# Moving small bound, epsilon and fold instructions between ScalarE, VectorE and GpSimd in a top-k attention kernel with a gated feed-forward

## The chip, the cores and the metric

The kernel runs on one core of one Trainium2 chip. The metric is the time of one execution in microseconds, as the device measures it. The kernel before took 1493.38 us (the median of three runs, 1491.07 to 1494.66).

In profile lines PE is TensorE (PEld its weight loads), DVE is VectorE, ACT is ScalarE, POOL is GpSimd and SP is SyncE, which here only issues DMAs.

## The reference, cut to what matters

```python
# q, k, v: 8 batches, 8 heads, 576 positions, 64 per head (float32)
scores = scale * np.matmul(q, k.transpose(0, 1, 3, 2))       # scale = 1/8
kth = np.partition(scores, -32, axis=-1)[..., -32:-31]       # 32nd largest of each row
scores = np.where(scores >= kth, scores, -1000000000.0)
scores = scores - np.max(scores, axis=-1, keepdims=True)
attn = np.exp(scores)
attn = attn / (np.sum(attn, axis=-1, keepdims=True) + 1e-09)
attn_out = np.matmul(attn, v)
x = attn_out.transpose(0, 2, 1, 3).reshape(4608, 512)
h = x @ w_in                                                  # w_in 512 x 2048, float64
out = (h * np.cos(h)) @ w_out                                 # w_out 2048 x 512, float64
```

For each of 64 x 576 rows of scores the kernel needs two numbers: the row's largest score and its 32nd largest. The weights come as 64-bit floats, so each is two 32-bit words.

## The kernel before, in words

**Units and slots.** The 4608 rows are cut into 36 blocks of 128 tokens, and each block has four head pairs: 144 units, each a tile `s` of 128 rows x 2 heads x 576 scores. A loop over slots (line 815) issues the work by hand: in slot i unit i (`u`) is searched for its top 32, unit i-1 (`w`) is masked and exponentiated, unit i-2 (`x`) is sent through a transposing DMA, and in each second slot units i-4 and i-3 (`z`) are multiplied with v. Slots 0 to 8 are `early_slot`, which transposes on TensorE instead; slots 9 to 140 are `slot`; the rest are `last_slot`. The order in which a slot calls its functions is the order of each engine's queue.

**The search.** For all but the last two units a row is folded first: position p of the first 288 scores is paired with position p of the last 288. The larger of each pair goes to `rest` (`fold_high`, L242, VectorE, one input in PSUM), the lesser to `low`. GpSimd makes the lesser without comparing: `fold_sum` (L252) adds the two as integers and `fold_low` (L261) subtracts the larger. VectorE then takes the top 32 of `rest` in four rounds of MAX8 (L323) and MATCH_REPLACE8 (L326), and the top 16 of `low` in two rounds. In the next slot `merge_first` and `merge_second` (L311, L316) combine the two lists; after that the 32nd largest and the largest of a row stand side by side at the end of the tile `top`.

**Bounds, mask, exponentials.** `bounds(w)` on ScalarE makes `nb`, both numbers times -1/8 (L333), and `nd`, the difference of the two times 1/8 (L336, one instruction for each head). `mask` (L345) is a Prelu with bias `nb` and slope 2^100 below zero, so that every score under the 32nd largest goes far down. `exponentials` (L353) takes Exp with bias `nd` and sums each row into `den`; L358 adds 1e-9. In the next slot VectorE's `reciprocal` (L362) stands first in its queue, and GpSimd's `split` (L379, L381) copies the 16-bit halves of the exponentials and of the reciprocals to `halves`, which SP writes out (L389) and reads back transposed (L395) as `pT`. The early slots multiply by the reciprocal on GpSimd (L367) and transpose on TensorE.

**The weights.** They come in 32 chunks of 128 x 512 double words into tiles `st`, seven buffers shared with the feed-forward's `g`. `decode_first` (ScalarE) turns the high word to a float pattern (L130) and rounds the low word to an integer (L133); `decode_second` (VectorE, L141) shifts the pattern by three bits; `decode_third` (GpSimd, L151) adds the rounded low word. The last chunks are decoded in slots 9 to 13.

**The feed-forward.** `feed` puts matmuls of `ff1` (L497) and `ff2` (L572) between the attention's matmuls on TensorE, on a budget of about four groups a slot. ScalarE takes their PSUM banks (L511, L513, L582) and computes the sine (L552); GpSimd reduces and gates (L533, L542, L559). `scale_values` (L451, VectorE) multiplies the attention's output by the reciprocals in each second slot.

Of the kernel before, what the change touches and what calls it, by code (L numbers as in the profile page):

```python
# [30 lines left out]
def kernel(  # L31
# [34 lines left out]
    nc.vector.memset(halfpi, math.pi / 2.0)  # L66
    quarter = consts.tile([P, 1], F32, tag="quarter")
    nc.vector.memset(quarter, 0.25)
    eps = consts.tile([P, 1], F32, tag="eps")
    nc.vector.memset(eps, EPS)  # L70

# [52 lines left out]
    def decode_first(n):  # L124


        for _ in range(min(n, len(wq["loaded"]))):
            st, w = wq["loaded"].popleft()
            lo, hi = st[:, :, 0], st[:, :, 1]
            nc.scalar.activation(  # L130
                out=w, in_=hi.bitcast(F32), func=AF.Prelu, scale=2.0**-111, alpha=2.0**32
            )
            nc.scalar.mul(out=lo, in_=lo.bitcast(U32), mul=2.0**-29)  # L133
            wq["second"].append((st, w))

    def decode_second(n):

        for _ in range(min(n, len(wq["second"]))):
            st, w = wq["second"].popleft()
            wi = w.bitcast(I32)  # L140
            nc.vector.tensor_scalar(  # L141
                out=wi, in0=wi, scalar1=3, scalar2=None, op0=ALU.logical_shift_left
            )
            wq["third"].append((st, w))
# [92 lines left out]

    def fold_high(u):

        s, sc = u["s"], u.pop("sc")  # L240
        u["rest"] = work.tile([P, 2, S], F32, tag="rest", name="rest", bufs=1)
        nc.vector.tensor_tensor(  # L242
            out=u["rest"][:, :, HS:S], in0=sc[:, :, 0:HS], in1=s[:, :, HS:S], op=ALU.max
        )

    def fold_sum(u):

        if not u["folds"]:
            return
        s = u["s"].bitcast(I32)  # L250
        u["low"] = work.tile([P, 2, HS], F32, tag="low", name="low", bufs=1)
        nc.gpsimd.tensor_tensor(  # L252
            out=u["low"].bitcast(I32), in0=s[:, :, 0:HS], in1=s[:, :, HS:S], op=ALU.add
        )

    def fold_low(u):

        if not u["folds"]:
            return
        low = u["low"].bitcast(I32)  # L260
        nc.gpsimd.tensor_tensor(  # L261
            out=low, in0=low, in1=u["rest"][:, :, HS:S].bitcast(I32), op=ALU.subtract
        )

    tops = []
    for i in range(3):
        t = consts.tile([P, 2, TOPK, 2], F32, tag=f"top{i}", name=f"top{i}")
        nc.vector.memset(t[:, :, 0, 1], -NEG)
        tops.append(t)

# [2 lines left out]
    def topk_first(u, w):  # L273

        u["top"] = tops[u["n"] % len(tops)]
        merges = w and w["folds"]
        if merges:
            merge_first(w)
        if u["folds"]:
            fold_sum(u)  # L280
            fold_high(u)
            if u["n"] <= EARLY:
                fold_low(u)
        else:
            u["rest"] = work.tile([P, 2, S], F32, tag="rest", name="rest", bufs=1)
        if merges:
            merge_second(w)
        topk_round(u, 0)

    def topk_round(u, rnd):  # L290
# [36 lines left out]

    def bounds(u):

        ends = u.pop("top").rearrange("p j r i -> p j (r i)")  # L330
        ends = ends[:, :, 2 * TOPK - 2 :] if u["folds"] else ends[:, :, 2 * TOPK - 2 :: 2 - 2 * TOPK]
        nb = u["nb"] = small.tile([P, 2, 2], F32, tag="nb", name="nb")
        nc.scalar.mul(out=nb, in_=ends, mul=-SCALE)  # L333
        nd = u["nd"] = small.tile([P, 2], F32, tag="nd", name="nd")
        for j in range(2):
            nc.scalar.activation(  # L336
                out=nd[:, j : j + 1], in_=ends[:, j, 1:2], func=AF.Identity,
                bias=nb[:, j, 0:1], scale=SCALE,
            )

    def mask(u):

        s, nb = u["s"], u.pop("nb")
        for j in range(2):
            nc.scalar.activation(  # L345
                out=s[:, j], in_=s[:, j], func=AF.Prelu, bias=nb[:, j, 1:2], scale=SCALE, alpha=FAR
            )

    def exponentials(u):
        s, nd = u["s"], u.pop("nd")  # L350
        den = u["den"] = small.tile([P, 2], F32, tag="den", name="den")
        for j in range(2):
            nc.scalar.activation(  # L353
                out=s[:, j], in_=s[:, j], func=AF.Exp, bias=nd[:, j : j + 1], scale=1.0,
                accum_out=den[:, j : j + 1],
            )

        nc.scalar.activation(out=den, in_=den, func=AF.Identity, bias=eps, scale=1.0)  # L358

    def reciprocal(u):  # L360
        u["rden"] = small.tile([P, 2], F32, tag="rden", name="rden")
        nc.vector.reciprocal(u["rden"], u.pop("den"))  # L362

    def normalise(u):
        s, rden = u["s"], u.pop("rden")
# [293 lines left out]
    def early_slot(i, u, w):  # L659
        n = 3 if i < 6 else 2  # L660
        topk_first(u, w)
        if i == 0:
            decode_second(1)
        scores(units[i + 1])
        for load, b, hp in at_slot.get(i, []):
            load(b, hp)
        load_weights(n)
        if w:
            bounds(w)
# [24 lines left out]
        if w:  # L694
            values([w])
            take_values([w])
        feed(2)
        sines(2)
# [7 lines left out]
    def slot(i, u, w, x, z):  # L706
        if x:
            reciprocal(x)
        if u:
            topk_first(u, w)  # L710
            decode_second(2)
        if x:
            send(x)
        if u:
            fold_low(u)
            topk_round(u, 1)
            topk_round(u, 2)
            topk_round(u, 3)
        made = scored.get(i, [])
        if z:  # L720
            take_banks()
        feed(1)

        ahead = i < EARLY + 5 * NP
        if z and not ahead:
            values(z)
        for m in made:
            scores(m)
        if z and ahead:
            values(z)  # L730


        late = len(made) > 0

        decoding = i < EARLY + 8
        if i % 2 and not decoding:
            sines(1)
        if w:
            bounds(w)
# [24 lines left out]
        if decoding or i == LAST:  # L764
            sines(1)

    def last_slot(i, u, w, x, z):
        if x:
            reciprocal(x)
        if u:  # L770
            topk_first(u, w)
            fold_low(u)
            topk_round(u, 1)
        bounds(w)
# [101 lines left out]
```

## Time and profile before

| what | value |
|---|---|
| median of three runs | 1493.38 us (1491.07 to 1494.66) |
| the profiled execution's own time | 1492.78 us |
| its span, first to last instruction | 1491.0 us |
| TensorE busy | 1409.2 us, 95% of the span |
| VectorE busy | 1332.0 us, 89% |
| ScalarE busy | 1217.2 us, 82% |
| GpSimd busy | 1165.1 us, 78% |
| mean granted TensorE clock | 0.981 |

A line of the groups gives the line in the code, the engine, the operation, what it writes and reads, the number of instructions, their busy time in us and the mean ns of one, then the idle time before them and what ended it. A line of the waits reads "engine, tile and line <- what released it: us in total, times, longest". A line of the timeline gives the start in us, the length in us, engine, line and operation, and in brackets the idle time before it with its releaser. A busy share is a mean over stages, and the stages differ here: the first 235 us fill the pipeline and decode the weights, the next 1140 us repeat one pattern every two slots, and the last 115 us empty it.

### The profile page before, as it was taken

What the parts mean: (1) busy time and instruction counts of PE and PEld (TensorE: products, weight loads), DVE (VectorE), ACT (ScalarE), POOL (GpSimd) and SP (SyncE); (2) the same over time, 40 slices, a digit from 0 to 9 for tenths busy, and PEclk for the clock granted to TensorE, in tenths of its full rate; (3) what the DMA queues carried; (4) which work ended last, traced back from release to release, by engine and by line L of the source; (5) the groups of instructions that cost most, each with busy time, mean ns of one, the idle gap of its engine ahead of it and who ended that gap; (6) DMA issues with size and microseconds to landing.
All of it is one profiled execution on the core that took longest, in us unless ns stands there. A gap on an engine that the chain in (4) does not pass through costs nothing.

```text
span 1491.0 us, 30595 instructions
## 1 busy us (share of the span) xinstructions
PE 1409.2 (95%) x10360; PEld 1013.3 (68%) x10360; DVE 1332.0 (89%) x4764; ACT 1217.2 (82%) x2438; POOL 1165.1 (78%) x822
## 2 busy tenths in 40 slices
PE   5678599999999999999999999999999999999998
PEld 3456366777777777777767777677667777777665
DVE  6888899999999999999999999999999999999721
ACT  6887778888888888888888888888888888888651
POOL 5688777888888888888888888888888888888410
PEclk9888799999999999999999999999999999999999
DMA  8523476656665566556655566656765566555200
GB/s 265 159 86 101 138 203 160 156 146 187 190 165 149 149 176 192 160 151 193 180 165 149 149 179 175 171 149 160 198 170 146 149 165 181 160 147 148 70 8 15
DMA packets 405549, 229.54 MB, mean 154 GB/s; under 512 B 355088, under 2 KB 371728, under 8 KB 405392
## 3 DMA queue, kind: packets, MB, share of 16 engines
q1 hardware_dynamic: 399984, 217.93, 53.8%
q10 hardware_dynamic: 5408, 9.65, 1.8%
q8 instruction: 82, 1.34, 0.4%
q14 instruction: 75, 0.61, 0.1%
HBM read 45.09 MB, written 95.94 MB: 95 GB/s over the span
## 4 chain that ended last, share of the span: by engine, by line
PE 76%; ACT 12%; DVE 5%; DMA 4%; issue 1%; POOL 0%; SPq 0%; ACTq 0%; POOLq 0%
PE mm L497 29%; PE o L572 28%; PE rim L432 10%; PE sc L223 7%; DMA pT<-rows 2%; ACT s L353 2%; DVE top L323 2%; PE rim L223 2%; ACT s L345 2%; ACT s L233 1%; DVE rest L326 1%; ACT L353 1%; ACT L552 1%; ACT x L552 1%; DVE xT L451 1%
## 5 line engine op out<-in xcount | busy, mean ns | idle before, releaser
L497 PEld LDWEIGHTS mm<-xT,w_in 128*128 128x128 f32 x4608 | 538.2, 192 | 74.5 <-issue 51.4
L572 PE MATMUL o<-w_out,g 128*128 128x512 f32 x1152 | 540.4, 603 | 17.2 <-POOL w_out L151 13.6
L497 PE MATMUL mm<-xT,w_in 128*128 128x128 f32 x4608 | 542.1, 276 | 6.2 <-DVE xT L451 2.8
L323 DVE MAX8 top<-rest 128x8 f32<-128x288 f32 x1148 | 470.3, 451 | 0.0
L326 DVE MATCH_REPLACE8 rest<-top,rest 128x288 f32<-128x288 f32 (+1 forms) x860 | 376.3, 445 | 0.0
L252 POOL TENSOR_TENSOR low<-s 128x576 int32<-128x576 int32 x142 | 204.4, 1439 | 197.5 <-DVE top L323 81.1
L572 PEld LDWEIGHTS o<-w_out,g 128*128 128x128 f32 x1152 | 203.1, 191 | 205.0 <-issue 181.3
L379 POOL COPY halves<-s 128x2304 uint16<-128x2304 uint16 x132 | 278.1, 2107 | 0.5 <-DMA rows<-halves 0.5
L353 ACT ACTIVATE s<-s,nd 128x576 f32<-128x576 f32 x288 | 220.3, 766 | 14.0 <-ACT ob L582 13.2
L323 DVE MAX8 top<-low 128x8 f32<-128x288 f32 x568 | 229.1, 445 | 0.0
L345 ACT ACTIVATE s<-s,nb 128x576 f32<-128x576 f32 x288 | 205.3, 760 | 0.0
L261 POOL TENSOR_TENSOR low<-low,rest 128x576 int32<-128x576 int32 x142 | 201.2, 1417 | 1.8 <-DVE top L316 0.9
L432 PEld LDWEIGHTS rim<-pT,v 128*64 128x64 f32 x2560 | 135.0, 141 | 66.3 <-ACT nb L333 43.2
L432 PE MATMUL rim<-pT,v 128*64 128x128 f32 (+1 forms) x2560 | 163.9, 273 | 16.4 <-ACT pT L413 8.4
L511 ACT ACTIVATE g<-mm 128x512 f32<-128x512 f32 x144 | 84.6, 588 | 114.5 <-PE mm L497 114.5
L559 POOL TENSOR_TENSOR g<-g,x 128x1024 f32<-128x1024 f32 x68 | 160.7, 2363 | 8.2 <-ACT x L552 8.2
L542 POOL TENSOR_TENSOR x<-g,x 128x1024 f32<-128x1024 f32 x68 | 160.8, 2365 | 5.7
L223 PE MATMUL sc<-k,q 64*128 64x448 f32 (+1 forms) x640 | 155.0, 594 | 7.5 <-DVE rest L326 5.5
L233 ACT COPY s<-sc 128x896 f32<-128x896 f32 x144 | 129.8, 901 | 3.2 <-PE sc L223 3.2
L326 DVE MATCH_REPLACE8 low<-top,low 128x288 f32<-128x288 f32 x284 | 123.5, 441 | 0.0
L242 DVE TENSOR_TENSOR rest<-sc,s 128x576 f32<-128x576 f32 x142 | 106.1, 747 | 11.4 <-ACT s L234 11.4
L223 PEld LDWEIGHTS rim<-k,q 64*128 64x128 f32 (+1 forms) x640 | 59.6, 184 | 56.7 <-issue 53.4
(56 smaller groups left out, 1394.3 us busy)
## 6 DMA issues: line engine op xcount, KB each, us to landing
rows<-halves SPq DMA_DIRECT2D x132, 640.0 KB, 3.0
out_dram<-ob ACTq DMA_DIRECT2D x36, 256.0 KB, 2.1
q<-in_q_dram SPq DMA_DIRECT2D x31, 288.0 KB, 3.5
st<-in_moe_w_in_dram SPq DMA_DIRECT2D x16, 512.0 KB, 5.7
v<-in_v_dram SPq DMA_DIRECT2D x32, 256.0 KB, 3.1
st<-in_moe_w_out_dram SPq DMA_DIRECT2D x16, 512.0 KB, 4.1
k<-in_k_dram SPq DMA_DIRECT2D x31, 144.0 KB, 3.7
k<-in_k_dram SPq DMA_DIRECT2D x32, 128.0 KB, 3.6
```

The lines of the kernel that those rows point to most:

```text
L223: nc.tensor.matmul(to[r0 : r0 + rows, j, 0 : k1 - k0], st["q"][d, q0 : q0 + rows], st["k"][d, k0:k1], start=True, stop=True,)
L252: nc.gpsimd.tensor_tensor(out=u["low"].bitcast(I32), in0=s[:, :, 0:HS], in1=s[:, :, HS:S], op=ALU.add)
L261: nc.gpsimd.tensor_tensor(out=low, in0=low, in1=u["rest"][:, :, HS:S].bitcast(I32), op=ALU.subtract)
L323: nc.vector.max(to[:, j], src[:, j])
L326: nc.vector.match_replace(rest[:, j], to[:, j], src[:, j], NEG)
L345: nc.scalar.activation(out=s[:, j], in_=s[:, j], func=AF.Prelu, bias=nb[:, j, 1:2], scale=SCALE, alpha=FAR)
L353: nc.scalar.activation(out=s[:, j], in_=s[:, j], func=AF.Exp, bias=nd[:, j : j + 1], scale=1.0, accum_out=den[:, j : j + 1],)
L379: nc.gpsimd.tensor_copy(out=halves[:, :, 0 : 2 * S], in_=s.rearrange("p (k h) -> p h k", h=2))
L432: nc.tensor.matmul(o[d, to], lhsT, rhs, start=c == 0, stop=c == NT)
L497: nc.tensor.matmul(mm[:, at : at + w], w_in[f // FC][:, c, (f % FC) * P : (f % FC + 1) * P], blk["xT"][:, c], start=c == 0, stop=c == NC - 1,)
L542: nc.gpsimd.tensor_tensor(out=x, in0=g, in1=x, op=ALU.subtract)
L572: nc.tensor.matmul(o, g[:, at : at + P], w_out[f], start=f == 0, stop=f == NF - 1)
```

## The change

Five things change.

1. `bounds` moves from ScalarE to VectorE: one TENSOR_REDUCE with negation writes minus the two numbers (`less`, four values a row) behind the end of `top`, and a second adds the 32nd largest and minus the largest (`nd`). For the two unfolded units a copy of one value a head goes ahead. It is called in `topk_first`, after `merge_second`, instead of ahead of `mask`.
2. `mask` on ScalarE first multiplies `nd` by 1/8, then does its two Prelu with scale 1 and bias `less`; the factor 1/8 moves to the Exp's scale.
3. Epsilon lies beside each row's sum in three fixed tiles `dens`; VectorE's `reciprocal` adds the two by a TENSOR_REDUCE ahead of the reciprocal. ScalarE's L358 goes.
4. The low word of the weights is rounded by a GpSimd TENSOR_SCALAR in `decode_second`, instead of ScalarE's L133 in `decode_first`.
5. For units 0 to 8 the lesser scores are made by one VectorE minimum, `fold_now`, instead of GpSimd's `fold_sum` and `fold_low`.

```diff
@@ decode_first / decode_second
-            nc.scalar.mul(out=lo, in_=lo.bitcast(U32), mul=2.0**-29)
...
+            nc.gpsimd.tensor_scalar(
+                out=lo, in0=lo.bitcast(U32), scalar1=2.0**-29, scalar2=1.0, op0=ALU.mult, op1=ALU.mult
+            )
             nc.vector.tensor_scalar(
                 out=wi, in0=wi, scalar1=3, scalar2=None, op0=ALU.logical_shift_left
             )
@@ folds
+    def fold_now(u):
+        s, sc = u["s"], u.pop("sc")
+        u["low"] = work.tile([P, 2, HS], F32, tag="low", name="low", bufs=1)
+        nc.vector.tensor_tensor(
+            out=u["low"], in0=sc[:, :, 0:HS], in1=s[:, :, HS:S], op=ALU.min
+        )
...
+    dens = []
+    for i in range(3):
+        t = consts.tile([P, 2, 2], F32, tag=f"dens{i}", name=f"dens{i}")
+        nc.vector.memset(t[:, :, 1], EPS)
+        dens.append(t)
@@ topk_first
         if u["folds"]:
-            fold_sum(u)
+            if u["n"] > EARLY:
+                fold_sum(u)
             fold_high(u)
-            if u["n"] <= EARLY:
-                fold_low(u)
...
         if merges:
             merge_second(w)
+        if w:
+            bounds(w)
+        if u["folds"] and u["n"] <= EARLY:
+            fold_now(u)
         topk_round(u, 0)
@@ bounds, mask, exponentials, reciprocal
-        nc.scalar.mul(out=nb, in_=ends, mul=-SCALE)
-        nd = u["nd"] = small.tile([P, 2], F32, tag="nd", name="nd")
-        for j in range(2):
-            nc.scalar.activation(
-                out=nd[:, j : j + 1], in_=ends[:, j, 1:2], func=AF.Identity,
-                bias=nb[:, j, 0:1], scale=SCALE,
-            )
+        if not u["folds"]:
+            nc.vector.tensor_copy(out=top[:, :, end - 1], in_=top[:, :, 0])
+        u["less"] = top[:, :, end : end + 2]
+        nc.vector.tensor_reduce(
+            out=u["less"], in_=top[:, :, end - 2 : end].unsqueeze(3), axis=mybir.AxisListType.X,
+            op=ALU.max, negate=True,
+        )
+        u["nd"] = small.tile([P, 2], F32, tag="nd", name="nd")
+        nc.vector.tensor_reduce(
+            out=u["nd"], in_=top[:, :, end - 1 : end + 1], axis=mybir.AxisListType.X, op=ALU.add
+        )
...
+        nc.scalar.mul(out=u["nd"], in_=u["nd"], mul=SCALE)
         for j in range(2):
             nc.scalar.activation(
-                out=s[:, j], in_=s[:, j], func=AF.Prelu, bias=nb[:, j, 1:2], scale=SCALE, alpha=FAR
+                out=s[:, j], in_=s[:, j], func=AF.Prelu, bias=less[:, j, 1:2], scale=1.0, alpha=FAR
             )
...
-        nc.scalar.activation(out=den, in_=den, func=AF.Identity, bias=eps, scale=1.0)
...
-        nc.vector.reciprocal(u["rden"], u.pop("den"))
+        den = small.tile([P, 2], F32, tag="den", name="den")
+        nc.vector.tensor_reduce(out=den, in_=u.pop("den"), axis=mybir.AxisListType.X, op=ALU.add)
+        nc.vector.reciprocal(u["rden"], den)
```

More of the change, by code (lines that the diff above doesn't have):

```diff
@@ L68 @@
     nc.vector.memset(quarter, 0.25)
-    eps = consts.tile([P, 1], F32, tag="eps")
-    nc.vector.memset(eps, EPS)
     DECODE = moe_w_in.dtype != F32
@@ L128, in decode_first @@
             st, w = wq["loaded"].popleft()
-            lo, hi = st[:, :, 0], st[:, :, 1]
+            hi = st[:, :, 1]
             nc.scalar.activation(
@@ L139, in decode_second @@
             st, w = wq["second"].popleft()
-            wi = w.bitcast(I32)
+            wi, lo = w.bitcast(I32), st[:, :, 0]
+            nc.gpsimd.tensor_scalar(
+                out=lo, in0=lo.bitcast(U32), scalar1=2.0**-29, scalar2=1.0, op0=ALU.mult, op1=ALU.mult
+            )
             nc.vector.tensor_scalar(
@@ L238, in fold_high @@
     def fold_high(u):
-        s, sc = u["s"], u.pop("sc")
+        s, sc = u["s"], u["sc"]
+        if u["n"] > EARLY:
+            del u["sc"]
         u["rest"] = work.tile([P, 2, S], F32, tag="rest", name="rest", bufs=1)
@@ L263, in fold_low @@
         )
+    dens = []
[3 more added lines that the diff above has]
+        dens.append(t)
     tops = []
     for i in range(3):
-        t = consts.tile([P, 2, TOPK, 2], F32, tag=f"top{i}", name=f"top{i}")
+        t = consts.tile([P, 2, TOPK + 1, 2], F32, tag=f"top{i}", name=f"top{i}")
         nc.vector.memset(t[:, :, 0, 1], -NEG)
@@ L279, in topk_first @@
         if u["folds"]:
-            fold_sum(u)
+            if u["n"] > EARLY:
+                fold_sum(u)
             fold_high(u)
-            if u["n"] <= EARLY:
-                fold_low(u)
         else:
@@ L328, in bounds, with mask @@
     def bounds(u):
-        ends = u.pop("top").rearrange("p j r i -> p j (r i)")
-        ends = ends[:, :, 2 * TOPK - 2 :] if u["folds"] else ends[:, :, 2 * TOPK - 2 :: 2 - 2 * TOPK]
-        nb = u["nb"] = small.tile([P, 2, 2], F32, tag="nb", name="nb")
-        nc.scalar.mul(out=nb, in_=ends, mul=-SCALE)
-        nd = u["nd"] = small.tile([P, 2], F32, tag="nd", name="nd")
+        top = u.pop("top").rearrange("p j r i -> p j (r i)")
+        end = 2 * TOPK
+        if not u["folds"]:
[9 more added lines that the diff above has]
+        )
+    def mask(u):
+        s, less = u["s"], u.pop("less")
+        nc.scalar.mul(out=u["nd"], in_=u["nd"], mul=SCALE)
         for j in range(2):
             nc.scalar.activation(
-                out=nd[:, j : j + 1], in_=ends[:, j, 1:2], func=AF.Identity,
-                bias=nb[:, j, 0:1], scale=SCALE,
-            )
-    def mask(u):
-        s, nb = u["s"], u.pop("nb")
-        for j in range(2):
-            nc.scalar.activation(
-                out=s[:, j], in_=s[:, j], func=AF.Prelu, bias=nb[:, j, 1:2], scale=SCALE, alpha=FAR
+                out=s[:, j], in_=s[:, j], func=AF.Prelu, bias=less[:, j, 1:2], scale=1.0, alpha=FAR
             )
@@ L350, in exponentials @@
         s, nd = u["s"], u.pop("nd")
-        den = u["den"] = small.tile([P, 2], F32, tag="den", name="den")
+        den = u["den"] = dens[u["n"] % len(dens)]
         for j in range(2):
             nc.scalar.activation(
-                out=s[:, j], in_=s[:, j], func=AF.Exp, bias=nd[:, j : j + 1], scale=1.0,
-                accum_out=den[:, j : j + 1],
+                out=s[:, j], in_=s[:, j], func=AF.Exp, bias=nd[:, j : j + 1], scale=SCALE,
+                accum_out=den[:, j, 0:1],
             )
-        nc.scalar.activation(out=den, in_=den, func=AF.Identity, bias=eps, scale=1.0)
     def reciprocal(u):
         u["rden"] = small.tile([P, 2], F32, tag="rden", name="rden")
-        nc.vector.reciprocal(u["rden"], u.pop("den"))
+        den = small.tile([P, 2], F32, tag="den", name="den")
+        nc.vector.tensor_reduce(out=den, in_=u.pop("den"), axis=mybir.AxisListType.X, op=ALU.add)
+        nc.vector.reciprocal(u["rden"], den)
     def normalise(u):
@@ L668, in early_slot @@
         if w:
-            bounds(w)
             mask(w)
@@ L738, in slot @@
         if w:
-            bounds(w)
             mask(w)
@@ L773, in last_slot @@
             topk_round(u, 1)
-        bounds(w)
+        if not u:
+            bounds(w)
         mask(w)
```

## The prediction

> **What bounds the kernel now.** I read the busy slices of the page first, then the windows, then VectorE's timeline, then the waits.
>
> ```profile
> PE   5678599999999999999999999999999999999998
> DVE  6888899999999999999999999999999999999721
> 150.00:175.00 25.00, 11.42 (x68) 5.50 (x68) 19.22 (x59) 18.13 (x35) 18.20 (x13) 0.72 0.52 144
> 400.00:500.00 100.00, 100.00 (x718) 72.45 (x717) 96.26 (x356) 88.34 (x175) 86.84 (x60) 1.00 0.57 158
> ```
>
> The slices show three stages: a fill in which TensorE lacks work, a long repetition, a short end. In a window the numbers after the length are busy us of PE, PEld, DVE, ACT and POOL. From 400 to 500 us TensorE is busy all the time, so it sets the pace there; but VectorE has 3.7 us free in 100. How near that is shows in two slots of VectorE's timeline:
>
> ```profile
> 1374.31 0.17 DVE L362 RECIPROCAL rden<-den 128x2 f32<-128x2 f32 x1 [0.75 <-ACT den L358]
> 1374.39 0.20 DVE L311 TENSOR_REDUCE top<-top 128x34 f32<-128x68 f32 x1
> 1374.51 0.75 DVE L242 TENSOR_TENSOR rest<-sc,s 128x576 f32<-128x576 f32 x1
> 1375.17 0.18 DVE L316 TENSOR_REDUCE top<-top 128x2 f32<-128x34 f32 x1
> 1375.29 0.82 DVE L323 MAX8 top<-rest 128x8 f32<-128x288 f32 x2
> ...
> 1383.05 0.47 DVE L451 TENSOR_TENSOR xT<-xT,pT 128x128 f32<-128x128 f32 x2
> 1383.44 0.15 DVE L362 RECIPROCAL rden<-den 128x2 f32<-128x2 f32 x1
> ```
>
> The reciprocals start a slot. The one before these is at 1364.75, so the pair of slots takes 1383.44 - 1364.75 = 18.69 us, and VectorE's only pause in it is the 0.75 us ahead of 1374.31. Its work per pair, every instruction at its start-to-start distance, is two slots of 8.73 (the length of slots without pause and without L451, as the one from 204.22 to 212.94) and 0.40 for L451: 17.86 us. So VectorE can take 0.83 us more per pair, 0.41 per slot, before it is slower than TensorE. I listed the reciprocals' starts from 237.03 to 1374.31: 60 pairs, 1137.28 us, mean 18.95; 28 pairs take 18.69 or 18.70, nine 18.77 to 18.90, three 17.87 (VectorE without pause, each followed by a pair over 20.2), and the others about 19 to 20.9, where TensorE has two-part units or waits for a transposed tile.
>
> ```profile
> DVE rden L362 <- ACT den L358: 72.9, 67, 7.4
> POOL low L252 <- DVE top L323: 81.1, 56, 3.4
> PE o L572 <- POOL w_out L151: 13.6, 2, 9.8
> ```
>
> The first wait is VectorE's slack, once a pair. The second matters for who pays if VectorE is late: GpSimd's fold_sum waits for VectorE to give `low` free, and behind it in GpSimd's queue stand `split`, the DMAs and TensorE's multiplication with v, which even now meets its tile with 0.2 us of waiting (at 619.28). Lateness of VectorE thus reaches TensorE almost at once. The third is the fill's largest stall, the last two chunks of w_out.
>
> [...] L311 at 605.53 takes 0.20 us while L252 runs, but the pair of L451 at 164.70 takes 3.43 us instead of 0.47 beside L252 and L379. [...] Reduces that do not need each other follow quickly: L316 to MAX8 above, 0.12 us. At 1393 `merge_second` stands directly behind `merge_first`, whose result it reads:
>
> ```profile
> 1393.23 0.22 DVE L311 TENSOR_REDUCE top<-top 128x34 f32<-128x68 f32 x1
> 1393.48 0.19 DVE L316 TENSOR_REDUCE top<-top 128x2 f32<-128x34 f32 x1
> 1393.59 1.41 DVE L323 MAX8 top<-s 128x8 f32<-128x576 f32 x2
> ```
>
> 0.25 us apart: its whole 0.22 plus 0.03.
>
> **VectorE's bill, per slot.** `less` reads what `merge_second` wrote, `nd` reads `less`, the reciprocal reads the new sum: three such waits. From 68 elements in 0.20 us and 34 in 0.18 I estimate 0.155 for a reduce of four. merge_second to less 0.18 + 0.03 = 0.21; less to nd 0.185; nd to the next, which is independent, 0.085 (the reciprocal's 0.08 above); minus the 0.12 that stood there: +0.36. The sum's reduce ahead of the reciprocal 0.155 + 0.03: +0.185. Together 0.55. Bounds: 0.27 if all three follow at 0.08 to 0.09 without waiting, 0.72 if each waiting step takes L311's 0.25.
>
> **ScalarE, per slot.** nb to mask took 0.61 us (607.71 to 608.32); one small multiply, at nb's distance of 0.22, replaces it: -0.39. L358 goes: -0.20 (38.65 to 38.85). It ends VectorE's pause of 0.75, but TensorE, at 100%, cannot use it. The bounds are ready 0.4 us later than now; ScalarE came to them 1.2 us after `merge_second` (607.71 against 606.49), which hides it.
>
> **Repetition.** VectorE's pair becomes 17.86 + 2 x 0.55 = 18.96 against TensorE's 18.69. Short pairs stretch: 28 x 0.27 = 7.6, the nine others 1.0; the three of 17.87 and their neighbours average over 18.96 and stretch by nothing, nor do the longer ones. **+8.5 us.** Reserve kept from long pairs could hide part; at 0.2 us of play I take none.
>
> **Fill.** In early slots 2 to 4 VectorE works 9.95 us of 11.1 and waits 1.2 for ScalarE. ScalarE loses up to three L133 at 0.57 us and 0.59 of small work, so it no longer sets the pace. But VectorE gains fold_now at L242's 0.66 and the 0.55: 9.95 + 1.21 = 11.16. So nothing is won there. Slots 5 to 8 took 11.9, 12.9, 10.9 and 11.4 with two chunks and with L141 blocked by GpSimd (2.1 us for two at 94.77, 0.76 unblocked); with L252 and L261 gone about 11.2, 10.8, 10.7, 10.7: -3.7, and slot 1, which waits 2.44 for ScalarE's decoding, -0.7. Holding `sc` for fold_now costs nothing: TensorE is still on the values (until 45.96, fold_high done 44.66).
>
> In slots 9 to 13 the new multiply has no row. L533's 1024 elements took 1.05 us, L367's 576 0.79; I take 0.75 for 512, bounds 0.5 and 1.4 (an add of 512 takes 1.30). Two per slot stand in GpSimd's queue ahead of `split` and fold_low and wait for the chunk's DMA, as at 153.3 us, where GpSimd had begun the slot at 149.44. `split` is followed on SP's queue by the halves' write, the transposing read and only then the next chunk's load (149.37, behind the read of 146.40), and ScalarE's L130 waits 5.4 us for that. So the multiplies delay the last chunks by 1.5 us in two slots; ScalarE wins back 0.57 a chunk. Of 4.4 us won I leave half: **-2 us**, between -6 and +3.
>
> **End.** From 1383 on the chain runs over ScalarE's nb and nd three times (0.6 each, now 0.22): **-1 us**. The copies and reduces of the unfolded units lie in VectorE's pauses (4.58 us at 1403.80); without cover they are 0.5 us.
>
> **Sum.** 1492.78 of the profiled execution - 2 + 8.5 - 1 = 1498.3; the median of the runs lies 0.6 above that execution: **1499 us**.
>
> **Rivals.** (1) The small reduces run without waiting, faster than before: then +0.27 a slot, VectorE's pair is 18.40 and TensorE keeps 18.69; the fill wins 2 us more, and 1493.4 - 4 - 1 gives 1488.5. For it: reduces beside other work cost 0.12. Against: the 0.25 at 1393. It decides at 0.41 us per slot. (2) The lag is carried over to the long pairs: 60 x 18.96 is 1138, what they take now; with -3 elsewhere 1491, no change. For it: every long pair has 1 to 2.7 us of VectorE pause. Against: fold_sum waits for VectorE 56 times. (3) ScalarE, which has only 0.14 us idle in odd slots, is what holds the pair, and its relief shortens it: TensorE's 100% speaks against; up to 1485. (4) GpSimd's multiplies stall the last chunks more than I count and each step costs 0.25: 19.3 per pair, +20 in the repetition, +3 in the fill: 1514.
>
> **Chances.** Forecast 0.62, (1) 0.13, (2) 0.14, (3) 0.03, (4) 0.08. 0.2%, about 3 us, is what a measurement of this kernel can tell. Slower by more 0.70, within 0.14, faster 0.16. The range 1488 to 1512 reaches down to (1) and up to most of (4); the forecast's own is 1496.5 to 1508.
>
> **What would show it.** Right: reciprocal starts 18.9 to 19.1 us apart per pair, VectorE without pause, 0.18 to 0.21 us between the reduces, the wait for ScalarE's sum gone, TensorE near 98.5% from 400 to 500 us; chunks decoded at about the same time as now. Wrong: pairs of 18.69 with pauses of VectorE left (1), VectorE full and the end unchanged (2), or w_out's stall grown by several us (4).

## The result, and the profile after

The changed kernel takes 1504.22 us (median of four runs, 1502.13 to 1508.02) beside 1492.79 for the kernel before (a fourth run added to the three known): ratio 1.0079, interval 1.0055 to 1.0103. It is slower, as forecast, but the time is 5 us above the 1499 forecast, so the loss of 11.4 us is twice the 5.6 that were forecast.

I count the reciprocals of VectorE from zero. "Pair n" is the two slots that begin at reciprocal n; the fill ends at reciprocal 18, the repetition at 138, and the end runs from there to ScalarE's last copy of the output (some 5 us of each execution lie outside the three). The profiled executions compare as follows, and the change is there twice more, as two further profiles:

| us | fill | repetition | end | profiled execution |
|---|---|---|---|---|
| before | 237.03 | 1137.28 | 113.55 | 1492.78 |
| changed | 236.59 | 1150.53 | 112.15 | 1504.25 |
| changed, second | 237.22 | 1154.78 | 112.14 | 1509.05 |
| changed, third | 237.48 | 1151.88 | 112.17 | 1506.55 |
| forecast against before | -2 | +8.5 | -1 | |

The whole loss lies in the repetition. The changed kernel's page gives the share of each engine in the chain that ended last, and the busy slices; the window from 400 to 500 us is the one shown of before.

```profile
DVE 63%; PE 22%; ACT 6%; DMA 5%; issue 2%; POOL 1%; SPq 1%; POOLq 0%; DVEq 0%; ACTq 0%
...
PE   4778599999999999999999999999999999999899
DVE  7998899999999999999989999999999998999931
...
400.00:500.00 100.00, 99.72 (x711) 71.79 (x710) 98.96 (x381) 80.59 (x142) 86.14 (x59) 1.00 0.56 158
```

Before, TensorE made 76% of that chain and VectorE 5%. Now VectorE makes 63%: the bound has changed engines. In the window VectorE is busy for 98.96 us of 100 (96.26 before) and ScalarE has 7.8 us less to do, which TensorE could not use. Each normal pair takes 18.94 us (slots of 9.67 and 9.27), where 18.69 was the rule. VectorE's timeline shows what it does at the start of a slot (start us, length us):

```profile
740.57 0.14 DVE L385 TENSOR_REDUCE den<-dens 128x2 f32<-128x4 f32 x1
740.75 0.17 DVE L386 RECIPROCAL rden<-den 128x2 f32<-128x2 f32 x1
...
741.61 0.18 DVE L335 TENSOR_REDUCE top<-top 128x2 f32<-128x34 f32 x1
741.83 0.16 DVE L354 TENSOR_REDUCE top<-top 128x4 f32<-128x4 f32 x1
742.02 0.16 DVE L359 TENSOR_REDUCE nd<-top 128x2 f32<-128x4 f32 x1
742.09 0.81 DVE L342 MAX8 top<-rest 128x8 f32<-128x288 f32 x2
```

Sum to reciprocal 0.18 us, `merge_second` to `less` 0.22, `less` to `nd` 0.19, and `nd` to the independent MAX8 only 0.07. Less the 0.12 that stood between L335 and MAX8 before, this is 0.18 + 0.48 - 0.12 = 0.54 us per slot. Whole slots without pause agree: 17.91 us a pair before (9.18 + 8.73), 18.94 now, 0.52 per slot.

In the waits, the 72.9 us for ScalarE's sum ahead of the reciprocal are gone; VectorE's wait at the same place, now for the sums at L376, is 10.6 us. Three lines answer to those shown of before:

```profile
DVE den L385 <- ACT s L376: 10.6, 13, 4.5
POOL low L262 <- DVE den L385: 119.3, 55, 4.5
...
PE o L596 <- POOL w_out L151: 15.9, 2, 8.9
```

GpSimd's fold_sum waits longest for VectorE's first reduce of the slot, 119.3 us (the longest of its waits before was 81.1, also for VectorE), and the stall for the last chunks of w_out has grown from 13.6 to 15.9.

**Where the 13.25 us of the repetition come from.** I set its 60 pairs against the same pairs of before:

| pairs, by their time before | number | changed | second | third |
|---|---|---|---|---|
| 18.6 to 18.75 us | 33, 34, 34 | +8.20 | +8.48 | +8.43 |
| 18.75 to 18.95 | 9 | +0.81 | +0.78 | +0.81 |
| 17.87, and the long ones (13, 11, 13) | 16, 14, 16 | -2.56 | -0.42 | +1.08 |
| over 22 us now | 2, 3, 1 | +6.81 | +8.66 | +4.28 |
| sum | | +13.25 | +17.50 | +14.60 |

(A pair over 22 us that was in another row before is counted only in the last.) The first two rows are the mechanism of the forecast, the same in all three to 0.3 us. The last row was not in it: pairs of 22 to 25 us, which the profile of before does not have. Pair 72 of the first profile is one. SP's queue beside two waits that follow from it, and one line of a normal slot to compare with:

```profile
734.66 0.34 SPq L413 DMA_DIRECT2D rows<-halves  x1
740.02 3.06 SPq L419 DMA_TRANSPOSE pT<-rows  x1
743.17 0.53 SPq L199 DMA_DIRECT2D v<-in_v_dram  x1
...
745.59 1.38 SPq L204 DMA_DIRECT2D v_tail<-in_v_dram  x2
747.01 0.58 SPq L413 DMA_DIRECT2D rows<-halves  x1
...
756.94 1.97 PE L456 MATMUL rim<-pT,v 128*64 128x128 f32 x16 [2.65 <-DMA pT<-rows]
...
762.47 0.49 DVE L475 TENSOR_TENSOR xT<-xT,pT 128x128 f32<-128x128 f32 x2 [3.28 <-ACT xT L463]
...
777.30 1.04 PE L456 MATMUL rim<-pT,v 128*64 128x128 f32 x16
```

The transposing read stands 5.4 us behind the write whose landing it needs; the loads of v stand behind the read; the next write, whose halves were ready at 744.31, stands behind the loads. Its tile reaches TensorE 2.65 us late, and VectorE, now the bound, pauses 3.28 us. Pair 124 begins the same way, but there the loads behind the late read, of q and k, are themselves late (write 1235.27, read 1240.08, loads from 1242.95, scores waiting for k until 1247.24, VectorE waiting 3.49 us). Late landings are no product of the change: 19 of 132 reads stood over 4 us behind their write before, 16 after. What the change seems to take away is the time to catch up.

The wait is only part of such a pair. The 16 matmuls at 756.94 take 1.97 us, those of the normal slot 1.04. The last three numbers of a window line are the granted TensorE clock, the DMA share and GB/s:

```profile
757.00:760.00 3.00, 3.00 (x22) 2.44 (x24) 2.19 (x8) 0.00 (x0) 1.72 (x1) 0.50 0.08 31
1248.50:1251.50 3.00, 3.00 (x6) 1.31 (x5) 2.93 (x13) 1.18 (x2) 1.11 (x1) 0.50 0.23 48
```

From 756.96 to 760.38 TensorE was granted half its clock, and again from 1248.48 to 1251.90, where it had just waited for k. The repetition of before has no such stretch. The three profiles of the change have two, three and two, each of 3.4 or 6.8 us, beginning late in a pause of TensorE of 1.5 to 3.6 us or up to 1.7 us behind it. What TensorE lost by it is by my estimate at most half of the part of each stretch behind the pause: 3.4, 6.0 and 5.0 us in the three profiles, beside 6.8, 8.7 and 4.3 in the last row of the table (in the third, one stretch lies in a pair of 21.45 us). So the unforeseen loss is not the wait alone; about half of it or more may be the lower clock. The experiments come back to it.

### The profile page after: what moved, and what is told of

It reads as the page before. It is cut to its first block, busy times and chain, and to the rows that moved or that the text cites. A ratio compares the mean times of both kernels' runs of the same rounds, so it can differ in the third digit from the quotient of the medians.

```text
span 1502.3 us, 30590 instructions
## 1 busy us (share of the span) xinstructions
PE 1414.7 (94%) x10360; PEld 1015.1 (68%) x10360; DVE 1392.8 (93%) x5209; ACT 1096.0 (73%) x1974; POOL 1162.0 (77%) x836
## 4 chain that ended last, share of the span: by engine, by line
DVE 63%; PE 22%; ACT 6%; DMA 5%; issue 2%; POOL 1%; SPq 1%; POOLq 0%; DVEq 0%; ACTq 0%
DVE top L342 28%; DVE rest L345 17%; PE mm L521 9%; PE o L596 8%; DVE low L345 6%; DVE rest L244 5%; PE rim L456 3%; DMA pT<-rows 3%; PE sc L223 2%; DVE xT L475 2%; ACT s L376 1%; DVE top L354 1%; DVE top L330 1%; DVE nd L359 1%; DMA v<-in_v_dram 1%
## 5 line engine op out<-in xcount | busy, mean ns | idle before, releaser
L596 PE MATMUL o<-w_out,g 128*128 128x512 f32 x1152 | 541.8, 604 | 19.1 <-POOL w_out L151 15.9
L262 POOL TENSOR_TENSOR low<-s 128x576 int32<-128x576 int32 x133 | 192.6, 1448 | 198.5 <-DVE den L385 119.3
L376 ACT ACTIVATE s<-s,nd 128x576 f32<-128x576 f32 x288 | 220.6, 768 | 14.0 <-ACT ob L606 13.2
L368 ACT ACTIVATE s<-s,top 128x576 f32<-128x576 f32 x288 | 206.1, 766 | 0.0
L271 POOL TENSOR_TENSOR low<-low,rest 128x576 int32<-128x576 int32 x133 | 188.3, 1416 | 0.6 <-DVE top L335 0.5
L223 PE MATMUL sc<-k,q 64*128 64x448 f32 (+1 forms) x640 | 157.1, 592 | 10.7 <-DMA k<-in_k_dram 10.2
L463 ACT COPY xT<-rim 128x256 f32<-128x256 f32 (+1 forms) x78 | 27.8, 357 | 128.0 <-PE rim L223 104.2
```

The costliest lines, as they stand in the source:

```text
L223: nc.tensor.matmul(to[r0 : r0 + rows, j, 0 : k1 - k0], st["q"][d, q0 : q0 + rows], st["k"][d, k0:k1], start=True, stop=True,)
L262: nc.gpsimd.tensor_tensor(out=u["low"].bitcast(I32), in0=s[:, :, 0:HS], in1=s[:, :, HS:S], op=ALU.add)
L271: nc.gpsimd.tensor_tensor(out=low, in0=low, in1=u["rest"][:, :, HS:S].bitcast(I32), op=ALU.subtract)
L368: nc.scalar.activation(out=s[:, j], in_=s[:, j], func=AF.Prelu, bias=less[:, j, 1:2], scale=1.0, alpha=FAR)
L376: nc.scalar.activation(out=s[:, j], in_=s[:, j], func=AF.Exp, bias=nd[:, j : j + 1], scale=SCALE, accum_out=den[:, j, 0:1],)
L596: nc.tensor.matmul(o, g[:, at : at + P], w_out[f], start=f == 0, stop=f == NF - 1)
```

## The experiments

Each was run beside the kernel before, on the same chip.

| kernel | us, median | ratio to before | fill | repetition | end |
|---|---|---|---|---|---|
| GpSimd's rounding and `fold_now` alone | 1494.58 | 0.9998 [0.9988, 1.0009] | 237.73 | 1138.95 | 111.97 |
| bounds and epsilon alone | 1501.13 | 1.0045 [1.0029, 1.006] | 232.41 | 1149.14 | 110.54 |
| before, with three such reduces added | 1516.63 | 1.0145 [1.0115, 1.0176] | 241.04 | 1156.83 | 114.06 |
| the change, reduces moved apart | 1486.57 | 0.9948 [0.993, 0.9967] | 234.57 | 1137.57 | 112.09 |
| bounds and epsilon alone, moved apart | 1482.38 | 0.993 [0.9905, 0.9955] | 232.41 | 1131.97 | 110.55 |
| the change without GpSimd's rounding, moved apart | 1481.33 | 0.9926 [0.9907, 0.9945] | 233.53 | 1132.16 | 110.59 |
| the change, epsilon left on ScalarE | 1492.44 | 0.9999 [0.9987, 1.0011] | 234.12 | 1140.61 | 111.34 |
| the change, loads issued by ScalarE | 1539.25 | 1.0308 [1.0261, 1.0356] | 238.24 | 1185.80 | 112.16 |
| the change, again | 1508.36 | 1.0076 [1.0049, 1.0104] | 237.22 | 1154.78 | 112.14 |
| the change, v loaded ahead of the read | 1500.80 | 1.0042 [1.0028, 1.0055] | 236.32 | 1146.65 | 110.53 |
| last of the "moved apart" with v loaded ahead | 1480.82 | 0.9907 [0.9889, 0.9924] | 231.93 | 1129.07 | 110.58 |

**1. Each half of the change.** GpSimd's rounding and `fold_now` alone (bounds, mask, exponentials and reciprocal as before):

```diff
-            nc.scalar.mul(out=lo, in_=lo.bitcast(U32), mul=2.0**-29)
+            nc.gpsimd.tensor_scalar(out=lo, in0=lo.bitcast(U32), scalar1=2.0**-29, ...)
...
+        if u["folds"] and u["n"] <= EARLY:
+            fold_now(u)
```

> The kernel before with the weights' low words rounded by GpSimd and the first nine units' lesser scores by VectorE, and with bounds and epsilon left on ScalarE. Theory (VectorE's three small reduces per slot, about 0.54 us, make it slower than TensorE in the repetition): no reduces, so pairs of slots are back at 18.69 us with a VectorE pause of about 0.75, and VectorE does not lose the fill's lead of some 4 us in slots 11 to 15; 1487 to 1490 us against 1492.8. Rival (GpSimd's multiply ahead of the split, or the fold moved to VectorE, is what costs the 11 us): 1500 us or more, the w_out stall longer.

The pairs are back at 18.69, so this half has no part in the loss. But the fill gains nothing either: 1.9 us ahead at reciprocal 7, the next four slots then take 62.04 us instead of 59.82. The time equals that of before, 4.6 us above the range I expected; 2.2 of these are the kernel before itself, which took 1495.01 us on that chip.

The other half alone, bounds and epsilon:

```diff
+        if w:
+            bounds(w)
         topk_round(u, 0)
...
-        nc.scalar.activation(out=den, in_=den, func=AF.Identity, bias=eps, scale=1.0)
+        nc.vector.tensor_reduce(out=den, in_=u.pop("den"), axis=mybir.AxisListType.X, op=ALU.add)
```

> Bounds and epsilon alone on VectorE; low words on ScalarE and all folds on GpSimd as before. Theory: pairs of 18.94 us, VectorE without pause, some 5 us of stretch in the repetition plus none, one or two stalls of 4 us at SP's queue; the fill wins a little less than in the full change: 1499 to 1507 us. Rival (the multiply or the fold costs it): 1490 to 1494.

Pairs of 18.94 and a repetition of 1149.14: this half makes the whole loss of the repetition. The fill is 4.6 us shorter than before, and 4.2 shorter than with both halves, where I had expected it to win a little less: here the first half costs.

**2. The same reduces without the change.** The kernel before, with three reduces of the same sizes in the same places; their results are not used, or are copies:

```diff
+        if w:
+            ballast(w)          # two reduces, the second reads the first
         topk_round(u, 0)
...
+        nc.vector.tensor_reduce(out=c, in_=u.pop("den").unsqueeze(2), ...)
-        nc.vector.reciprocal(u["rden"], u.pop("den"))
+        nc.vector.reciprocal(u["rden"], c)
```

> The kernel before with three small VectorE reduces added at the change's places, each reading what the one in front wrote, results of the first two unused, the third a copy of the sums that the reciprocal reads. ScalarE and GpSimd keep all their work. Theory: VectorE's time alone makes the loss: pairs of 18.94 us, 1497 to 1507 us, and as ScalarE is not relieved, not faster than the change by more than 3 us. Rival (the loss comes from the moved work's place: bounds ready later, GpSimd's queue): 1491 to 1495.

Pairs of 18.93: the reduces alone set the pair, whatever ScalarE does. It came out slower than I expected, with the fill 4.0 us longer and two pairs of 25.6 and 22.3, which have 10.2 us at half the clock. ScalarE keeps all its work here (86.98 us in the window). The normal pairs stretch as in the change (+8.12 for the short ones), but the long ones, without those over 22 us, give back only 1.5 us, where they give back 5.7 with bounds and epsilon moved from ScalarE. That points to ScalarE's relief as what shortens the long pairs; the part on rival (3) sets all versions side by side.

**3. The same work without the waits.** The full change, with other instructions set between each reduce and the one whose result it needs: the reciprocal goes behind `merge_first`, `less` and `nd` between the first instructions of the search. No instruction is added or left out.

```diff
     def search(to, src, rest, more, between=()):
         for j in range(2):
             nc.vector.max(to[:, j], src[:, j])
+            if j < len(between):
+                between[j]()          # bound(w), then distance(w)
...
+            add_eps(x)                # reciprocal's reduce; the reciprocal after merge_first
```

> The full change with the same three reduces, moved so that none reads what the instruction in front of it wrote: the two of the bounds behind the first and second MAX8 of the first round, the sums' reduce ahead of merge_first and the reciprocal behind it. Theory: each then costs 0.08 to 0.09 us, 0.26 a slot, VectorE's pair is 17.86 + 0.52 = 18.4 and TensorE's 18.69 counts again: 1486 to 1491 us. Rival (it is not the waits between dependent reduces; a small reduce costs its whole 0.16 us anywhere): pairs of 18.8 to 18.9, 1497 to 1503.

VectorE's timeline:

```profile
742.42 0.16 DVE L397 TENSOR_REDUCE den<-dens 128x2 f32<-128x4 f32 x1 [0.34 <-ACT s L385]
742.50 0.22 DVE L330 TENSOR_REDUCE top<-top 128x34 f32<-128x68 f32 x1
742.62 0.16 DVE L401 RECIPROCAL rden<-den 128x2 f32<-128x2 f32 x1
...
743.85 0.14 DVE L360 TENSOR_REDUCE top<-top 128x4 f32<-128x4 f32 x1
743.90 0.45 DVE L342 MAX8 top<-rest 128x8 f32<-128x288 f32 x1
744.27 0.14 DVE L368 TENSOR_REDUCE nd<-top 128x2 f32<-128x4 f32 x1
744.33 0.08 DVE L347 MATCH_VALUE_LOAD rest<-top,rest 128x8 f32 x1
```

A reduce of the same length (0.14 to 0.16 us) now costs 0.05 to 0.08 from its start to the next start. Two slots without pause take 18.31 us (9.32 + 8.99), so 0.20 more per slot than before, not 0.52; VectorE pauses again (the 0.34 at 742.42), and the pairs are 18.69. The sign of the change turns: 0.9948. Nothing but the order on VectorE differs, so the waits between dependent instructions are shown to be the cause.

**4. The point from which it decides.** The forecast put it at 0.41 us per slot (0.39 by the 17.91 of whole slots). With epsilon left on ScalarE and the other reduces in their dependent places, VectorE gains 0.36:

```diff
+        nc.scalar.activation(out=den, in_=den, func=AF.Identity, bias=eps, scale=1.0)
...
-        nc.vector.tensor_reduce(out=den, in_=u.pop("den"), axis=mybir.AxisListType.X, op=ALU.add)
-        nc.vector.reciprocal(u["rden"], den)
+        nc.vector.reciprocal(u["rden"], u.pop("den"))
```

> The full change with its reduces in their places, but epsilon added by ScalarE as before, so that VectorE gains 0.36 us a slot and not 0.55. My theory, with its threshold of 0.41 us a slot: VectorE's pair is 17.86 + 0.72 = 18.58 us, less than TensorE's 18.69; pairs of 18.69 with about 0.1 us of pause, repetition 1137 to 1143 us, time 1489 to 1494. If instead the later bounds themselves set the pair (a chain from the bounds over ScalarE to the next slot), the pairs stay at 18.85 to 18.95 and the time at 1499 to 1504.

Pairs of 18.69; in the fill's slots without other waits a pair takes 18.63 (9.54 + 9.09), 0.06 under TensorE's. The window:

```profile
400.00:500.00 100.00, 100.00 (x720) 72.73 (x719) 99.05 (x375) 82.64 (x153) 85.46 (x59) 1.00 0.57 159
```

VectorE's 99.05 is no less than in the changed kernel (98.96), yet TensorE is back at 100.00 and the time at that of before. Which engine has the longer pair decides, and the busy share alone could not have told.

**5. What costs in the fill.** Bounds and epsilon moved apart, first without the other half, then with `fold_now` but the rounding on ScalarE:

```diff
@@ both, against the change moved apart
-            nc.gpsimd.tensor_scalar(out=lo, in0=lo.bitcast(U32), scalar1=2.0**-29, ...)
+            nc.scalar.mul(out=lo, in_=lo.bitcast(U32), mul=2.0**-29)
@@ the first only
-            fold_now(u)
+                fold_low(u)      # and fold_sum, on GpSimd
```

> The bounds and epsilon on VectorE with the small reduces moved apart, the low words left on ScalarE and fold_low left on GpSimd. My theory: VectorE's pair is 18.3 to 18.4 us as in the full change moved apart, so the pairs are 18.69; the fill wins what the bounds alone won (4.6 us at the nineteenth slot) and some 1 to 2 us more, as VectorE no longer loses 0.5 us a slot; time 1480 to 1485, below the full change moved apart. The rival, that rounding by GpSimd and fold_now bring something of their own once VectorE has slack again, expects 1486 to 1490.

> The full change with the reduces moved apart, but the low words multiplied by ScalarE as in the kernel before; fold_now stays on VectorE. If GpSimd's multiplication is what costs about 4 us in the fill: the fill as short as that of the bounds moved apart alone, 1480 to 1485. If it is fold_now on VectorE: as the full change moved apart, 1486 to 1488.

Both come to 1481 to 1482 us, below the 1486.57 with GpSimd's rounding; that one ran on another chip, and the intervals of the ratios overlap, so the profiles must tell. From reciprocal 7 to 11 the four slots take 56.82 us in the first and 57.12 in the second, 60.60 with GpSimd's rounding: 3.5 us. All versions with the bounds moved agree: 60.2 to 60.8 in the seven profiles with GpSimd's rounding, 56.7 to 57.1 in the four without. The place, in GpSimd's and SP's lines, with the rounding on GpSimd

```profile
137.06 1.45 POOL L138 TENSOR_SCALAR st<-st 128x512 int32<-128x512 uint32 x2
...
141.12 0.34 SPq L428 DMA_DIRECT2D rows<-halves  x1
...
147.10 0.52 SPq L115 DMA_DIRECT2D st<-in_moe_w_out_dram  x1
```

and on ScalarE:

```profile
137.10 2.31 POOL L416 COPY halves<-s 128x2304 uint16<-128x2304 uint16 x1
...
139.97 0.34 SPq L426 DMA_DIRECT2D rows<-halves  x1
...
145.88 0.52 SPq L115 DMA_DIRECT2D st<-in_moe_w_out_dram  x1
```

From the same start the two multiplications put off `split` by 1.5 us, and with it the write, the read and the load of the next chunk by 1.2. Not all of the 3.5 us is kept: in the next five slots the version with GpSimd's rounding takes 0.9 us less, and its whole fill is 2.2 and 1.0 us longer than the two others. Its repetition and end, 5.4 and 1.5 us longer than the second's, are another matter: they hold a pair of 25.1 us and stretches at half the clock, which the two others do not have. `fold_now` by itself is within what the runs can tell (1481.33 and 1482.38).

The repetition of both is over 5 us shorter than before: 0.0 us in the short pairs, -6.9 and -5.9 in the long ones, though VectorE has more to do than before.

**6. The pairs over 22 us.** First, the loads of q, k and v in the repetition issued from ScalarE's queue, so that none stands in SP's:

```diff
         for load, b, hp in at_slot.get(i, []):
-            load(b, hp)
+            load(b, hp, nc.scalar)     # its dma_start calls, instead of nc.sync's
```

> The full change, with the loads of q, k and v in the repetition issued from ScalarE's queue and not from SP's. If the two pairs of 23 us come from loads standing between a late transposing read and the next write of the halves in SP's queue: pairs of 18.94 as before, none over 21, repetition 1141 to 1144 us, time 1494 to 1498. If they come from the write landing late as such: pairs over 22 remain, time 1501 to 1506.

Much slower, with five pairs of 24 to 28 us, but not for the rival's reason: ScalarE itself stands still at L576, by my reading behind its issues (the wait below: total, times, longest).

```profile
ACT L576 <- issue: 66.5, 31, 9.8
```

The changed kernel has no such wait. The k load of 144 KB also takes a median of 4.7 us to land instead of 3.6 and that of 128 KB 6.1 instead of 3.5, while q's 288 KB take 3.4 in both; why k lands later was not shown. It is a different kernel in too many ways, and tells nothing on SP's order.

So the order alone was changed: v's loads between the write of the halves and the transposing read, where SP waits for the landing anyway. Beside it the changed kernel again, twice.

```diff
         write_halves(x)
+        for b, hp in vs:
+            load_v(b, hp)
         transposes(x)
```

> The full change, with the loads of v in the repetition put between the write of the halves and the transposing read, where SP's queue waits for the write to land anyway. If loads that stand between a late read and the next write make the pairs of 23 us: those with v (even slots, as 72) go, those with q and k stay, and the time falls by 2 to 5 us, to 1498 to 1502. If the late landing alone makes them, or the loads slow the write that they now run beside: no gain, 1502 to 1508.

> The changed kernel again, unaltered, for a further profile. If pairs of 22 us and more belong to the change (the slots with loads cannot give the lag back once VectorE has no pause): one to three of them, at the same long pairs (68, 72, 104 or 124), and the time 1501 to 1507. If the two that were seen were chance: none or one, and the profiled execution at 1494 to 1498.

> The changed kernel a third time, for its profile alone: as the one before it, one to three pairs of 22 us and more if they belong to the change, none or one if they are chance.

The change again is slower than before by the same ratio, 1.0076, at a time 1.4 us above the range I expected. The two further profiles have pairs over 22 us at 68, 104 and 124, and at 124: they belong to the change, though not always at the same place. With v's loads ahead of the read,

```profile
758.38 0.36 SPq L413 DMA_DIRECT2D rows<-halves  x1
758.83 1.31 SPq L199 DMA_DIRECT2D v<-in_v_dram  x1
...
763.74 2.78 SPq L419 DMA_TRANSPOSE pT<-rows  x1
767.73 0.37 SPq L413 DMA_DIRECT2D rows<-halves  x1
```

the next write follows the read at once. The time is 1500.80 us where the change beside it took 1508.36, and the repetition is 3.9 to 8.1 us shorter than in the three profiles of the change. The intervals of the two ratios still overlap, at 1.0049 to 1.0055. One pair remains (68, 24.5 us), and there eight loads of q and k stand between the read at 700.91 and the write at 708.72. The read stands over 4 us behind its write in 29 of 132 slots here, more often than in the change, as it now waits behind v's loads too. This speaks for SP's order as the way in which a late landing becomes a stall, but does not show it; why a write lands late in those slots stays open, as late landings were found with and without loads or output writes under way beside them (11 and 8 of the 19 before, 8 and 8 of the 16 in the changed kernel).

The half clock goes with these pairs everywhere. Leaving out the version with ScalarE's loads, the profiles have 13 pairs over 22 us, and each has a stretch at half the clock that lies in it or, in pair 124, reaches into it; one more stretch lies in the pair of 21.45. The four profiles without such a pair (before, the two of experiment 5 and that of experiment 7) have no stretch in their repetition. TensorE paused for 1.5 to 4.8 us at or ahead of the beginning of each. Yet a pause does not always bring it: before has three of 1.7, 2.0 and 1.8 us that none follows. What decides, I cannot tell. Nor is it settled how much reserve of VectorE prevents such a pair: the six profiles with pairs of 18.93 or 18.94 and SP's loads have one to three each; the seven with pairs of 18.69 have one in three of them and none in four.

**7. A version that beats both.** The same order of v's loads in the version with the reduces moved apart and the rounding on ScalarE:

> The reduces moved apart, the low words left on ScalarE, fold_now on VectorE, and the loads of v put between write and read. If the last of these removes a stall: 1477 to 1481; if it removes nothing: 1481 to 1485 as without it.

1480.82 us, 0.9907 of before. Against the same version without the moved loads (1481.33, on another chip) no difference can be told.

## Why the prediction was right or wrong

**The mechanism was right, and its price.** VectorE's bill was 0.55 us per slot and measured 0.54 by distances and 0.52 by whole slots; the pair was to be 18.96 and is 18.94. The reading that carried it was the pair of merges at 1393, where a reduce that needs the one in front took its whole length and 0.03; the three new waits are the median length of the reduce in front (0.15, 0.18 and 0.16 us) plus 0.03 each. In the lines shown a dependent instruction starts 0.18 to 0.22 us after the start of the reduce in front; an independent one starts 0.05 to 0.08 us after the start of a reduce of four, before that one's recorded end. The new reduces and `fold_now` were not held up anywhere: the three reduces took 0.13 to 0.16 us in all 144 slots, `fold_now` 0.75 us in all nine.

**Rival (1)** had the right point of decision: the version moved apart and the one without epsilon lie under it, at 18.69. It was wrong only in that the change as written does not run so. **Rival (2)**, that the lag is carried over to the long pairs, fell: without those over 22 us, they and the three fast ones together give back 2.6 and 0.4 us in two profiles and lose 1.1 in the third, of 9 us of lag. **Rival (3)** fell for the pair of 18.69, which no version got under, but perhaps not for the long pairs. Eleven of the long pairs stay under 22 us in every version with SP's loads. Summed, they are 3.0 to 5.9 us shorter than before in the seven profiles with bounds and epsilon off ScalarE and v's loads in their place, 1.7 and 2.0 in the two that left both on ScalarE (experiments 1 and 2), and 2.2 with epsilon alone left there. No version relieves ScalarE without giving VectorE the work, so this points to ScalarE and does not show it. I had set all of ScalarE's relief in the repetition at nothing, from TensorE's 100% in one window from 400 to 500 us. **Rival (4)** had the delay of the chunks in the right place, but not at 19.3 a pair.

**The steps that failed** are two terms of the sum.

- *The repetition, +8.5*: the stretch of the short and middle pairs was 9.0 (28 x 0.27 + 1.0 = 8.6 forecast). That it fits so well is in part luck: I had counted 28 pairs of 18.69 or 18.70 us where the profile of before has 34, and 34 x 0.27 + 1.0 would have been 10.2. But the term "the longer ones stretch by nothing" left out the pairs over 22 us, 4.3 to 8.7 in the three profiles. The lines for it were in the forecast: lateness of VectorE reaches TensorE through `split` and the DMAs. I followed it for its size in a normal slot and not for a slot in which loads stand in SP's queue behind a late landing, nor had I a term for the half clock after a pause.
- *The fill, -2*: measured -0.4, +0.2 and +0.5. The 4.4 us to be won by slot 9 were 4.1 in the first profile (3.2 and 2.3 in the others), and the delay of the multiplications, 1.5 us in two slots, was 3.5 in four by the comparison of the two versions moved apart. What was missing stands largely from reciprocal 11 to 16: five slots in which VectorE has no pause take 47.48 us instead of 44.89, +0.52 each. My fill ended with slot 13, which begins at reciprocal 11, and my repetition began at reciprocal 18, so nearly all of these 2.6 us were in neither sum.

The multiplication itself was put at 0.75 us and took 0.66 (mean of 32). The end's -1 measured -1.4 and stands: what blurs it is one more stretch of 3.4 us at half the clock, which some profiles have in the end ahead of the last copy and some not. Among those with it, before takes 113.55 and the change 112.15 (112.09 to 112.17 in five profiles with bounds and epsilon moved). Among those without, the half of experiment 1, with bounds and epsilon on ScalarE as before, takes 111.97, and the five with both moved 110.53 to 110.59: 1.4 us less both times.

TensorE was to be near 98.5% from 400 to 500 us and shows 99.72, although the pairs are 1.3% longer for the same matmuls, at a granted clock of 1.00 in that window as before. A busy TensorE is thus no sign that it sets the pace; the distance of the reciprocals was the better measure.

## What to carry to other kernels

Before work is given to an engine with slack, take that engine's time per period without its pauses and set it against the period of the engine that bounds: here 0.83 us in 18.69 was all there was, at a busy share of 96%. Price a small instruction from start to start, and as a dependent one where it stands behind the one it needs: here an independent instruction set between the two took the price from 0.5 to 0.2 us per slot and turned slower into faster. Apply a term per slot to every slot that the engine bounds, those between two stages too, and ask of lateness what it does in the slots in which loads share the queue. Look at the granted clock behind a long pause (here 0.50 for 3.4 or 6.8 us behind some) before its whole length is put down to the wait.

## What the runs showed of the hardware

- In the repetition TensorE's granted clock fell to 0.50 for 3.4 or 6.8 us at or behind the end of pauses of 1.5 to 4.8 us, and 16 matmuls took 1.97 us instead of 1.04; other pauses of 1.4 to 2.2 us were not followed by it.
- A VectorE reduce of four elements a row lasted a median of 0.15 or 0.16 us in the changed kernel and 0.14 to 0.16 in the lines of the version moved apart; counted from its start, an independent instruction started after 0.05 to 0.08 us, one that needed its result after a median of 0.18 or 0.19.
- GpSimd's multiplication of 128 x 512 from uint32 to int32 took 0.66 us, half of the 1.30 that its addition of 512 takes in the same kernel.
- A write of 640 KB to DRAM and the transposing read that needs it stood 3.1 us apart in the median, but over 4 us in 14% of the slots in the kernel before and in 12 to 17% in the three profiles of the changed one.
- With the loads of q, k and v issued from ScalarE's queue, ScalarE stood idle for 66.5 us in 31 places, up to 9.8 us at a time, in which it waited for nothing that the profile shows; the changed kernel has no such wait.
